# Early release of the first w_in columns, a split q normalisation and a later eighth block in a fused attention and feed-forward kernel

## The chip, the cores and the metric

The kernel runs on one core of one Trainium2 chip. Times are microseconds of the device (us); a lower time is better. The engines are named as in the profile: PE is TensorE, PEld its weight loads, DVE is VectorE, ACT is ScalarE, POOL is GpSimd, SP is SyncE, which here issues transfers only.

## What is computed

The reference is a linear attention followed by a feed-forward layer. q, k and v are (8 batches, 8 heads, 576 positions, 64) in f32; the result is (4608, 512) in f32.

```python
q_s = softmax(q, axis=-1)          # over the 64 of a head
k_s = softmax(k, axis=2)           # over the 576 positions
kv  = einsum('bhsd,bhse->bhde', k_s, v)
x   = einsum('bhsd,bhde->bhse', q_s, kv)   # then (4608, 512): positions x (heads, 64)
h   = x @ w_in                     # (4608, 2048)
g   = h + sin(alpha * h)**2 / (alpha + 1e-9)
out = g @ w_out                    # (4608, 512)
```

## The kernel before

**Tiles.** The 4608 rows are cut into nine tiles of 512 (index t), so a batch of 576 rows is one tile and an eighth; a batch is held as nine blocks j of 64 rows. The 2048 columns of w_in are 16 blocks ni of 128; the contraction over 512 has four steps ki. xT holds the attention's result transposed (four chunks c of 128 partitions), win and wout the weights in bf16.

**Attention of a batch.** `exp_q` and `exp_k` take the exponentials on ACT in two halves ii (line 117, 128 x 1152 each). `norm_q` sums q's exponentials (144), takes reciprocals (145) and multiplies (146); its list of engines says who multiplies which half, and sums and reciprocals are always DVE's. The normalised q is transposed: in batch 0 by PE through an identity matrix (186), with ACT copying the result to qT (325, 334, 335). `kv_mm` multiplies k's exponentials with v and a column of ones (157), `kv_norm` divides on DVE into kbd (167, 170), and `attn_chunk` (214) multiplies kbd with qT into xT, which ACT and DVE copy in turn (342).

**Feed-forward of a tile.** `h_slot` runs four matmuls for a block ni (234), the sine on ACT (240), the square on ACT (242), POOL (244) or DVE (246) by a string of letters, and the combination on DVE (250). Then `o_quad` (tile 0) or `o_stream` multiplies with wout (254) and copies out (260). Tile 0 starts with ki 0 and 1 of blocks 0 and 1, then goes on block by block. Its sixteen blocks take PSUM banks from two pools: four in ps_h, two lent by ps_e for blocks 2, 3, 8, 9, 14 and 15. o_quad's four accumulators take the four banks of ps_h, which the last ps_h blocks, 10 to 13, free; a ps_e tile asked for afterwards waits for block 14.

**What sets the order.** Each engine works through its own list in the order in which the code issues it, and waits for the others by semaphores; nothing is rescheduled. A transfer is started by the engine on which it is issued: SP for q, k, v, the results and (before) the first 256 columns of w_in, which come as f32 into a staging tile wf (280) and are cast by POOL (320). The other columns and w_out are issued by POOL, which casts in the transfer (107, 110). Staging tiles come from a pool of five.

**The head (before the first feed-forward matmul).** SP issues q, k, v of batch 0 and then wf's two halves, one behind the other (94, 275, 280). POOL waits for k's first half with a one-element copy called held (317), then issues six requests for w_in columns 256 to 1536, casts wf in one piece, and issues the rest. PE fills its waits with matmuls whose result is not used, `warm_up` (306): seven before batch 0's first transposes, six between the two groups of transposes. v is cast in four pieces by ACT and DVE (310). At the end of the head ACT loads the table for the sine (343).

**Around the end of tile 0.** o_quad's matmuls are drawn by `take(os, n)`. After ten of them PE computes block j 8 of batch 0 (`attn_chunk` into xp), ACT copies it (396), 36 more matmuls follow, and ACT's list goes on with batch 1's exponentials (the table for these is loaded first), then batch 1's norm_q with POOL and DVE, the k exponentials, the v casts (131) and so on.

Of the kernel before, what the change touches and what calls it, by code (L numbers as in the profile page):

```python
# [15 lines left out]
F32 = mybir.dt.float32  # L16
BF16 = mybir.dt.bfloat16
# [6 lines left out]
def kernel(  # L24
# [14 lines left out]
    nc = tc.nc  # L39
    ctx.enter_context(nc.allow_non_contiguous_dma(reason="layout"))  # L40
    B, H, S, D = q.shape
# [3 lines left out]
    J = 9  # L45
    P = S // J
# [7 lines left out]
    singles = ctx.enter_context(tc.tile_pool(name="singles", bufs=1))  # L54
    stage = ctx.enter_context(tc.tile_pool(name="stage", bufs=5))
    att1 = ctx.enter_context(tc.tile_pool(name="att1", bufs=1))
    att2 = ctx.enter_context(tc.tile_pool(name="att2", bufs=2))
# [9 lines left out]
    xT = singles.tile([128, 4, NT], BF16, name="xT")  # L67
    win = singles.tile([128, 4, d_ff], BF16, name="win")
# [7 lines left out]
    def src_view(t, b):  # L76
        return t[b].rearrange("(i e) (p j) d -> (e p) i (j d)", e=2, j=J)

    win_v = moe_w_in.rearrange("(x c d) n -> x d c n", x=2, c=4)
# [3 lines left out]
    staged = {}  # L83

    def load(name, t, b, halves=False, eng=nc.sync, gate=None):

        st = stage.tile([128, 4, J, D], F32, name=f"st_{name}", tag="st")
        for ii in range(2) if gate else ():
            gate(st[:, ii, 0, 0:1], zero)
        view = src_view(t, b)  # L90
        flat = st.rearrange("p i j d -> p i (j d)")
        if halves:
            for ii in range(2):
                eng.dma_start(out=flat[:, ii::2], in_=view[:, ii::2])  # L94
        else:
            eng.dma_start(out=flat, in_=view)
        staged[name, b] = st
# [6 lines left out]
    def load_win(c0, c1):  # L104
        n = slice(c0, c1)
        for x in range(2):
            nc.gpsimd.dma_start(out=win[64 * x:64 * x + 64, :, n], in_=win_v[x][:, :, n])

    def load_wout(c):
        nc.gpsimd.dma_start(out=wout[:, 4 * c:4 * c + 4, :], in_=wout_v[:, 4 * c:4 * c + 4, :])  # L110


    A = {}

    def exp_to(dst, src):
        for ii in range(2):
            nc.scalar.activation(dst[:, :, ii * 128:(ii + 1) * 128].rearrange("p j (x d) -> p x j d", x=2),  # L117
                                 src[:, ii::2], AX.Exp)

    def exp_q(b):  # L120
        A["qe", b] = att2.tile([128, J, 4 * D], BF16, name="qe")
        exp_to(A["qe", b], staged["q", b])

    def exp_k(b):
        A["ke", b] = att2.tile([128, J, 4 * D], BF16, name="ke")
        exp_to(A["ke", b], staged["k", b])

    def cast_v(b, engs):
        vv = vb[b % 2].rearrange("p j (i c) -> p i j c", i=4)
# [3 lines left out]
    def norm_q(b, engs):  # L133

        qe = A["qe", b].rearrange("p j (ii x d) -> p ii j x d", ii=2, x=2)
        A["qn", b] = qn = att1.tile([128, 2, J, 2 * D], BF16, name="qn")
        qs = small.tile([128, J, 4], F32, name="qs")
        if len(engs) == 1:
            nc.vector.tensor_reduce(qs, A["qe", b].rearrange("p j (i d) -> p j i d", i=4), axis=AXL.X, op=ALU.add)  # L139
            nc.vector.reciprocal(qs, qs)  # L140
        for ii in range(2):
            part = qs[:, :, 2 * ii:2 * ii + 2]
            if len(engs) == 2:
                nc.vector.tensor_reduce(part, qe[:, ii], axis=AXL.X, op=ALU.add)  # L144
                nc.vector.reciprocal(part, part)
            engs[ii % len(engs)].tensor_tensor(qn[:, ii].rearrange("p j (x d) -> p j x d", x=2), qe[:, ii],  # L146
                                               part.unsqueeze(3).to_broadcast([128, J, 2, D]), op=ALU.mult)
# [25 lines left out]
    def q_tile(b):  # L173
        if ("qT", b) not in A:
            A["qT", b] = att2.tile([128, 2, J, 128], BF16, name="qT")
        return A["qT", b]
# [6 lines left out]
    def q_transpose_ii(b, ii, j0, j1, tp):  # L183

        for j in range(j0, j1):
            nc.tensor.transpose(tp[:, j - j0], A["qn", b][:, ii, j], identb)
# [80 lines left out]
    ACT_CP, DVE_CP, GP_CP = nc.scalar.copy, nc.vector.tensor_copy, nc.gpsimd.tensor_copy  # L267
    V, GP = nc.vector, nc.gpsimd
# [5 lines left out]
    for ii, j0, j1 in VJ:  # L274
        nc.sync.dma_start(out=st[:, ii::2, j0:j1].rearrange("p i j d -> p i (j d)"),
                          in_=src_view(v, 0)[:, ii::2, j0 * D:j1 * D])

    wf = stage.tile([128, 4, J, D], F32, name="st_w", tag="st")[:, :, 0:4].rearrange("p c a b -> p c (a b)")
    for x in range(2):
        nc.sync.dma_start(out=wf[64 * x:64 * x + 64], in_=win_v[x][:, :, 0:256])  # L280
    make_identity(nc, ident)
    DVE_CP(identb, ident)
    zero = singles.tile([128, 1], F32, name="zero")
# [14 lines left out]
    nc.vector.reciprocal(inva_sb, alpha_sb)  # L298

    exp_q(0)  # L300
    exp_k(0)

    def warm_up(n):

        for _ in range(n):
            nc.tensor.matmul(warm, identb, A["qe", 0][:, 0:4, 0:128], start=True, stop=True)

    def cast_v0(ii, j0, j1, eng):
        vv = vb[0].rearrange("p j (i c) -> p i j c", i=4)
        eng(vv[:, 2 * ii:2 * ii + 2, j0:j1, 0:D], staged["v", 0][:, ii::2, j0:j1])  # L310


    warm_up(7)
    norm_q(0, [V, V])
    q_tile(0)

    GP_CP(singles.tile([128, 1], F32, name="held"), staged["k", 0][:, 0, 0, 0:1])
    for c0, c1 in ((256, 512), (512, 1024), (1024, 1536)):
        load_win(c0, c1)
    GP_CP(win[:, :, 0:256], wf)  # L320
    load_win(1536, 2048)
    for c in range(2):
        load_wout(c)
# [1 line left out]
    ACT_CP(A["qT", 0][:, 0, 0:8], tps[0])  # L325
    cast_v0(0, 0, 5, ACT_CP)
    cast_v0(0, 5, 9, DVE_CP)
    warm_up(6)
    q_transpose_ii(0, 1, 0, 8, tps[1])
    for ii in range(2):  # L330
        q_transpose_ii(0, ii, 8, 9, tps[2][:, ii:ii + 1])
# [7 lines left out]
    for c in range(4):  # L339
        xp = ps_h.tile([128, MF], F32, name="hp", tag="h")  # L340
# [4 lines left out]
    def h_slot(t, ni, sq, lag, wide=None):  # L345
        hp = mm_h(t, ni, wide, 2 if t < 2 and ni < 2 else 0)
        lag.append((t, ni, hp, sine(t, ni, hp, sq)))

    def flush(lag, keep):
        while len(lag) > keep:  # L350
            combine(*lag.pop(0))
# [14 lines left out]
    def take(it, n=1000):  # L366
        for _ in range(n):
            if next(it, 0) == 0:
                return
# [4 lines left out]
    with ES:  # L374
        def lent():
            return ps_e.tile([128, 2, MF], F32, name="hh", tag="a")[:, 0]

        late = {6: lambda: load("q", q, 1, halves=True, gate=DVE_CP), 8: lambda: load_wout(2),
                10: lambda: load_wout(3), 13: lambda: load("k", k, 1, halves=True, gate=DVE_CP)}
        for ki in range(2):  # L380
            for ni in range(2):
                mm_h(0, ni, lent, ki, ki + 1)
        for ni in range(nN):
            h_slot(0, ni, "DPAPPAPPAPPAPPAP"[ni], lag, lent)
            flush(lag, 1)
            if ni in late:
                late[ni]()
        flush(lag, 0)

        accs = [ps_h.tile([128, dm], F32, name="hp", tag="h") for _ in range(4)]  # L390
        os = o_quad(0, accs, [DVE_CP, ACT_CP, DVE_CP, ACT_CP])
        take(os, 10)
        xp = ps_e.tile([128, 4, P], F32, name="xp", tag="a")
        for c in range(4):
            attn_chunk(0, c, 8, 9, xp[:, c])
        ACT_CP(xT[:, :, 8 * P:9 * P], xp)
        take(os, 36)
        exp_q(1)
        load("v", v, 1, halves=True)
        load_batch(2)  # L400
        norm_q(1, [GP, V])
        exp_k(1)
        for ii in range(2):
            q_transpose(1, ii, ps_e, DVE_CP)
        cast_v(1, [ACT_CP, DVE_CP])
        nc.scalar.activation(zero, zero, AX.Sin)
        take(os, 8)
        kv_mm(1, 0, ps_e, split=True)
        kv_norm(1, 0, 1)
        take(os, 2)  # L410
        kv_mm(1, 1, ps_e, split=True)
        kv_norm(1, 1, 2)
        take(os, 1)

        c0 = J * P
        for ii in range(2):
            xp = ps_e.tile([128, 2, 512], F32, name="xp", tag="a")[:, :, 0:7 * P]
            for e in range(2):
                attn_chunk(1, 2 * ii + e, 0, 7, xp[:, e])
            (ACT_CP, DVE_CP)[ii](xT[:, 2 * ii:2 * ii + 2, c0:c0 + 7 * P], xp)  # L420
            take(os, 2)
        take(os)
        load("q", q, 3)
        load("k", k, 3)

        for ki in range(2):
            for ni in range(2):
                mm_h(1, ni, lent, ki, ki + 1)
        for ni in range(nN):
            h_slot(1, ni, SQ[ni], lag, lent)  # L430
            flush(lag, 1)
        cast_v(2, [GP_CP, GP_CP])
        flush(lag, 0)
# [17 lines left out]
    os = o_stream(1)  # L451
    take(os, 8)
    xp = ps_a.tile([128, 4, 2 * P], F32, name="xp", tag="a")
# [19 lines left out]
    for c in range(4):  # L473
        xp = ps_h.tile([128, MF], F32, name="hp", tag="h")[:, 0:6 * P]
# [3 lines left out]
    xp = ps_a.tile([128, 2, 512], F32, name="xp", tag="a")[:, :, 0:6 * P]  # L478
# [27 lines left out]
    for t in range(3, nT):  # L506
        b = t + 1 if t + 1 < B else None
        os = o_stream(t - 1)
# [59 lines left out]
```

The softmax here doesn't subtract the row's maximum and nothing guards it: scores larger than these inputs give would overflow.

## Time and profile before

| | us |
|---|---|
| median of five runs | 290.25 |
| the five runs | 289.45, 289.58, 290.25, 290.43, 290.51 |
| the profiled execution, its own time | 289.19 |
| its span (first to last instruction) | 287.4 |
| PE busy | 275.0 (96%) |
| ACT busy | 227.3 (79%) |
| DVE busy | 188.5 (66%) |
| POOL busy | 80.2 (28%) |
| line 234, 520 matmuls | 129.7 |
| line 254, 496 matmuls | 124.2 |

Times of single instructions come from the one profiled execution. A matmul's end is modelled, and matmuls overlap, so the distance between the starts of neighbours says more than the length of one. In a timeline line the columns are the start, the length, the engine, the line of the code, the operation, what it writes from what, and how many were merged; in brackets is the idle time before it and what ended it. In a line of waits they are the total, the number and the longest.

### The profile page before, as it was taken

The numbers are of one execution on the slowest core, as the hardware profiler recorded it, in microseconds if no ns is written. First come the engines' busy times: TensorE is split into PE (matmuls) and PEld (weight loads), VectorE is DVE, ScalarE is ACT, GpSimd is POOL, SyncE is SP. The second block draws the span as 40 slices with busy tenths as digits, with TensorE's granted clock in tenths as the row PEclk, the third lists the DMA queues.
The fourth block names the chain that finished last, engine by engine and source line by source line (L and its number), as shares of the span: only waits on it lengthen the run. The fifth ranks groups of instructions, "written<-read, shape, count | busy, mean of one in ns | idle before, by whom it ended". The sixth has DMA issues, their size and how long they took to land.

```text
span 287.4 us, 4262 instructions
## 1 busy us (share of the span) xinstructions
PE 275.0 (96%) x1570; PEld 130.4 (45%) x1570; DVE 188.5 (66%) x280; ACT 227.3 (79%) x321; POOL 80.2 (28%) x73
## 2 busy tenths in 40 slices
PE   1899999999999999999999999999999999999994
PEld 0434454445454445444544454445444444444443
DVE  3967596889958667856776677757674555555412
ACT  4799765999479999899889998999877777777500
POOL 0779420675775571005300440032000000000000
PEclk9999999999999999999999999999999999999998
DMA  7999999855899956129911990116011111111142
GB/s 253 339 203 237 271 392 407 284 197 168 189 181 410 364 185 125 38 44 366 277 34 23 329 334 6 38 39 138 17 39 37 37 37 39 37 38 37 46 104 73
DMA packets 37893, 46.03 MB, mean 160 GB/s; under 512 B 15968, under 2 KB 21360, under 8 KB 37872
## 3 DMA queue, kind: packets, MB, share of 16 engines
q1 hardware_dynamic: 33392, 41.69, 47.4%
q0 software_dynamic: 4288, 3.93, 8.4%
q8 instruction: 12, 0.20, 0.3%
q10 hardware_dynamic: 192, 0.14, 0.2%
q14 instruction: 9, 0.07, 0.1%
HBM read 36.71 MB, written 9.44 MB: 161 GB/s over the span
## 4 chain that ended last, share of the span: by engine, by line
PE 81%; DMA 5%; POOL 4%; DVE 3%; issue 2%; ACT 2%; SPq 2%; POOLq 0%
PE hp L234 35%; PE op L254 33%; PE hp L254 4%; POOL s L244 4%; DMA st_w<-in_moe_w_in_dram 3%; PE kvp L157 2%; ACT s L240 2%; PE xp L206 2%; PE hh L234 2%; DMA qT<-qn 1%; PE op L538 1%; PE op L234 1%; DVE g L250 1%; SPq L94 1%; DVE qs L144 1%
## 5 line engine op out<-in xcount | busy, mean ns | idle before, releaser
L250 DVE SCALAR_TENSOR_TENSOR g<-s,inva_sb,hp 128x512 bf16<-128x512 f32 x130 | 96.2, 745 | 64.2 <-ACT s L242 54.2
L234 PE MATMUL hp<-xT,win 128*128 128x512 bf16 x520 | 129.7, 379 | 0.3 <-POOL win L320 0.3
L254 PE MATMUL op<-wout,g 128*128 128x512 bf16 x496 | 124.2, 379 | 0.0
L240 ACT ACTIVATE s<-hp,alpha_sb 128x512 f32<-128x512 f32 x130 | 87.7, 683 | 25.4 <-PE hp L234 25.1
L234 PEld LDWEIGHTS <-win 128*128 128x128 bf16 x576 | 56.1, 98 | 68.0 <-POOL win L320 0.8
L254 PEld LDWEIGHTS <-g 128*128 128x128 bf16 x560 | 54.1, 98 | 61.4 <-issue 0.6
L242 ACT ACTIVATE s<-s 128x512 f32<-128x512 f32 x112 | 70.5, 630 | 3.6
L146 POOL TENSOR_TENSOR qn<-qe,qs 128x1152 bf16<-128x1152 bf16 x12 | 25.3, 2129 | 73.9 <-DVE qs L140 62.5
L244 POOL TENSOR_TENSOR s<-s 128x512 f32<-128x512 f32 x29 | 30.5, 1063 | 21.9 <-ACT s L240 21.4
L260 DVE COPY o<-op 128x512 f32<-128x512 f32 (+2 forms) x33 | 22.1, 669 | 9.5 <-PE op L254 7.1
L117 ACT ACTIVATE ke<-st_k 128x1152 bf16<-128x1152 f32 x16 | 17.9, 1151 | 3.0 <-DMA st_k<-in_k_dram 3.0
L117 ACT ACTIVATE qe<-st_q 128x1152 bf16<-128x1152 f32 x16 | 17.8, 1155 | 2.8 <-DMA st_q<-in_q_dram 2.8
L139 DVE TENSOR_REDUCE qs<-qe 128x36 f32<-128x2304 bf16 x5 | 12.8, 2553 | 8.7 <-ACT qe L117 8.6
L131 POOL CAST vb<-st_v 128x1152 bf16<-128x1152 f32 x12 | 13.6, 1163 | 10.4 <-DMA st_v<-in_v_dram 10.4
L254 PE MATMUL hp<-wout,g 128*128 128x512 bf16 x64 | 15.1, 379 | 0.0
L209 DVE CAST xT<-xp 128x512 bf16<-128x512 f32 (+1 forms) x18 | 13.4, 742 | 0.0
L144 DVE TENSOR_REDUCE qs<-qe 128x18 f32<-128x1152 bf16 x6 | 8.0, 1331 | 4.9 <-ACT qe L117 4.9
L117 ACT ACT_TABLE_LOAD x7 | 9.0, 1283 | 1.3 <-PEq L552 1.2
L157 PEld LDWEIGHTS <-ke 64*128 64x128 bf16 x288 | 8.2, 93 | 3.5 <-ACT s L242 1.3
L157 PE MATMUL kvp<-vb,ke 64*128 64x130 bf16 x288 | 9.7, 216 | 0.0
L234 PE MATMUL hh<-xT,win 128*128 128x512 bf16 x40 | 9.4, 379 | 0.0
L206 PE MATMUL xp<-qT,kbd 128*128 128x256 bf16 (+1 forms) x40 | 8.2, 286 | 0.4 <-DVE xT L209 0.3
(68 smaller groups left out, 116.9 us busy)
## 6 DMA issues: line engine op xcount, KB each, us to landing
out_dram<-o SPq DMA_DIRECT2D x70, 128.0 KB, 2.3
st_q<-in_q_dram SPq DMA_DIRECT2D x6, 1152.0 KB, 6.2
st_k<-in_k_dram SPq DMA_DIRECT2D x6, 1152.0 KB, 8.4
st_v<-in_v_dram SPq DMA_DIRECT2D x6, 1152.0 KB, 10.3
st_q<-in_q_dram SPq DMA_DIRECT2D x4, 576.0 KB, 5.6
st_k<-in_k_dram SPq DMA_DIRECT2D x4, 576.0 KB, 6.8
wout<-in_moe_w_out_dram POOLq DMA_DIRECT2D x4, 512.0 KB, 10.2
st_v<-in_v_dram SPq DMA_DIRECT2D x3, 576.0 KB, 9.5
```

What stands on the lines that cost most here:

```text
L117: nc.scalar.activation(dst[:, :, ii * 128:(ii + 1) * 128].rearrange("p j (x d) -> p x j d", x=2), src[:, ii::2], AX.Exp)
L131: engs[ii](vv[:, 2 * ii:2 * ii + 2, :, 0:D], staged["v", b][:, ii::2])
L146: engs[ii % len(engs)].tensor_tensor(qn[:, ii].rearrange("p j (x d) -> p j x d", x=2), qe[:, ii], part.unsqueeze(3).to_broadcast([128, J, ...
L157: nc.tensor.matmul(kvp[:, e, ii * 130:(ii + 1) * 130], ke[r, j, ii * 128:(ii + 1) * 128], vt[r, j, ii * 130:(ii + 1) * 130], start=(j == 0 ...
L206: nc.tensor.matmul(xp[:, e, 0:n], kt[:, e, ii], qT[:, ii, j0:j1, e * 64:(e + 1) * 64], start=True, stop=True)
L234: nc.tensor.matmul(hp, win[:, ki, ni * 128:(ni + 1) * 128], xT[:, ki, t * MF:(t + 1) * MF], start=(ki == 0), stop=(ki == 3))
L240: nc.scalar.activation(s, hp, AX.Sin, scale=alpha_sb[:, ni:ni + 1])
L242: nc.scalar.activation(s, s, AX.Square)
L244: nc.gpsimd.tensor_tensor(s, s, s, op=ALU.mult)
L250: nc.vector.scalar_tensor_tensor(G[t][:, ni], in0=s, scalar=inva_sb[:, ni:ni + 1], in1=hp, op0=ALU.mult, op1=ALU.add)
L254: nc.tensor.matmul(acc, G[t][:, ni, j * 128:(j + 1) * 128], wout[:, ni, :], start=(ni == 0), stop=(ni == nN - 1))
L260: eng(o[:, cols], acc)
```

## The change

Four edits in the head and one after tile 0:

- the two transfers of wf are no longer issued behind v: ACT writes one element of wf between the two halves of k's exponentials, and SP's transfers, which overwrite wf, wait for that. The copy held is gone, and POOL's requests for the other columns stand behind its share of norm_q;
- norm_q of batch 0 multiplies its first half on POOL and its second on DVE, instead of both on DVE;
- POOL casts wf in two pieces of 128 columns each;
- the warm-up matmuls are nine and one instead of seven and six;
- block j 8 of batch 0 comes after twenty matmuls of o_quad instead of ten, and DVE copies it instead of ACT; 26 follow instead of 36.

```diff
@@ -112,8 +112,8 @@
 
     A = {}
 
-    def exp_to(dst, src):
-        for ii in range(2):
+    def exp_to(dst, src, iis=(0, 1)):
+        for ii in iis:
             nc.scalar.activation(dst[:, :, ii * 128:(ii + 1) * 128].rearrange("p j (x d) -> p x j d", x=2),
                                  src[:, ii::2], AX.Exp)
 
@@ -121,9 +121,10 @@
         A["qe", b] = att2.tile([128, J, 4 * D], BF16, name="qe")
         exp_to(A["qe", b], staged["q", b])
 
-    def exp_k(b):
-        A["ke", b] = att2.tile([128, J, 4 * D], BF16, name="ke")
-        exp_to(A["ke", b], staged["k", b])
+    def exp_k(b, iis=(0, 1)):
+        if 0 in iis:
+            A["ke", b] = att2.tile([128, J, 4 * D], BF16, name="ke")
+        exp_to(A["ke", b], staged["k", b], iis)
 
     def cast_v(b, engs):
         vv = vb[b % 2].rearrange("p j (i c) -> p i j c", i=4)
@@ -276,8 +277,6 @@
                           in_=src_view(v, 0)[:, ii::2, j0 * D:j1 * D])
 
     wf = stage.tile([128, 4, J, D], F32, name="st_w", tag="st")[:, :, 0:4].rearrange("p c a b -> p c (a b)")
-    for x in range(2):
-        nc.sync.dma_start(out=wf[64 * x:64 * x + 64], in_=win_v[x][:, :, 0:256])
     make_identity(nc, ident)
     DVE_CP(identb, ident)
     zero = singles.tile([128, 1], F32, name="zero")
@@ -298,7 +297,12 @@
     nc.vector.reciprocal(inva_sb, alpha_sb)
 
     exp_q(0)
-    exp_k(0)
+    exp_k(0, (0,))
+
+    nc.scalar.copy(wf[:, 0, 0:1], zero)
+    exp_k(0, (1,))
+    for x in range(2):
+        nc.sync.dma_start(out=wf[64 * x:64 * x + 64], in_=win_v[x][:, :, 0:256])
 
     def warm_up(n):
 
@@ -310,14 +314,13 @@
         eng(vv[:, 2 * ii:2 * ii + 2, j0:j1, 0:D], staged["v", 0][:, ii::2, j0:j1])
 
 
-    warm_up(7)
-    norm_q(0, [V, V])
+    warm_up(9)
+    norm_q(0, [GP, V])
     q_tile(0)
-
-    GP_CP(singles.tile([128, 1], F32, name="held"), staged["k", 0][:, 0, 0, 0:1])
     for c0, c1 in ((256, 512), (512, 1024), (1024, 1536)):
         load_win(c0, c1)
-    GP_CP(win[:, :, 0:256], wf)
+    for n in range(2):
+        GP_CP(win[:, :, n * 128:n * 128 + 128], wf[:, :, n * 128:n * 128 + 128])
     load_win(1536, 2048)
     for c in range(2):
         load_wout(c)
@@ -325,7 +328,7 @@
     ACT_CP(A["qT", 0][:, 0, 0:8], tps[0])
     cast_v0(0, 0, 5, ACT_CP)
     cast_v0(0, 5, 9, DVE_CP)
-    warm_up(6)
+    warm_up(1)
     q_transpose_ii(0, 1, 0, 8, tps[1])
     for ii in range(2):
         q_transpose_ii(0, ii, 8, 9, tps[2][:, ii:ii + 1])
@@ -389,12 +392,12 @@
 
         accs = [ps_h.tile([128, dm], F32, name="hp", tag="h") for _ in range(4)]
         os = o_quad(0, accs, [DVE_CP, ACT_CP, DVE_CP, ACT_CP])
-        take(os, 10)
+        take(os, 20)
         xp = ps_e.tile([128, 4, P], F32, name="xp", tag="a")
         for c in range(4):
             attn_chunk(0, c, 8, 9, xp[:, c])
-        ACT_CP(xT[:, :, 8 * P:9 * P], xp)
-        take(os, 36)
+        DVE_CP(xT[:, :, 8 * P:9 * P], xp)
+        take(os, 26)
         exp_q(1)
         load("v", v, 1, halves=True)
         load_batch(2)
```

## The prediction

> **What bounds the kernel now.** I read the page first: PE is busy 96% of the span, so only what keeps PE waiting, and what PE does before its stream begins, can move the time. Then the list of PE's waits over the whole span (us in total, times, longest), without its first two lines, 3.1 and 2.8 for the first transfers:
>
> ```profile
> ...
> PE tp L186 <- DVE qn L146: 1.0, 1, 1.0
> PE hp L214 <- DVE kbd L170: 0.6, 2, 0.4
> PE hp L234 <- POOL win L320: 0.3, 1, 0.3
> PE xp L206 <- DVE xT L209: 0.3, 1, 0.3
> PE xp L214 <- DVE g L250: 0.3, 1, 0.3
> ```
>
> All but the last two lie in the head, before the first feed-forward matmul. The chain that ended last shows what starts that stream:
>
> ```profile
> 5.82 9.17 DMA st_w<-in_moe_w_in_dram
> ...
> 15.12 1.05 POOL win L320
> ...
> 16.22 1.90 PE hp L234 x8
> ```
>
> The first w_in columns land at 14.99, GpSimd casts them for 1.05, and PE starts at 16.22. From there it runs at one 512-column matmul per 0.216 us ((1.90 - 0.38) / 7), and the only waits left are 0.3 and 0.3. But the timeline shows a second chain just behind it:
>
> ```profile
> 14.88 0.59 ACT L342 CAST xT<-hp 128x512 bf16<-128x512 f32 x1 [0.15 <-PE hp L214]
> 15.27 1.36 DVE L342 CAST xT<-hp 128x512 bf16<-128x512 f32 x2
> ...
> 15.72 0.59 ACT L342 CAST xT<-hp 128x512 bf16<-128x512 f32 x1 [0.25 <-PE hp L214]
> ...
> 16.32 1.28 ACT L343 ACT_TABLE_LOAD   x1
> ```
>
> xT's four chunks are done at 15.47, 15.95, 16.31 and 16.63, so the columns are ahead of need by only half a microsecond. And ACT goes from its last copy straight into the sine table, then sines (the first at 17.73). The table of busy time by stretch (PE, PEld, DVE, ACT, POOL after the length) says that ACT is full in this stage:
>
> ```profile
> 25.00:30.00 5.00, 5.00 (x25) 2.25 (x23) 4.00 (x6) 4.80 (x8) 4.97 (x6) 1.00 1.15 294
> ```
>
> So the first tile has two limits: PE from 16.22, and ACT from 16.32, which nowhere in it waits for PE. They meet here:
>
> ```profile
> 30.05 2.42 PE L254 MATMUL hp<-wout,g 128*128 128x512 bf16 x10
> ...
> 32.75 0.28 PE L214 MATMUL xp<-qT,kbd 128*128 128x64 bf16 x4 [0.28 <-DVE g L250]
> ```
>
> Ten matmuls from 30.05 would be through the issue at 30.05 + 10 x 0.216 = 32.21; xp starts at 32.75. That is 0.54 lost: about 0.1 inside the ten (2.42 against 9 x 0.216 + 0.38 = 2.32: the fourth accumulator's bank, freed by the sine of column block 13), 0.44 for xp, whose buffer the combine of block 14 frees.
>
> **What the Trainium skill says.** GPSIMD Engine Reference, section 4.1: a two-input elementwise operation takes GpSimd about twice VectorE's time. Here the same multiplication takes 2.13 on POOL and 1.36 on DVE, a ratio of 1.6. Its section 1 says that GpSimd shares SBUF interfaces with VectorE, contended when DVE has two SBUF inputs. The trace agrees; line 146 on DVE alone, and beside POOL in batch 1:
>
> ```profile
> 7.83 1.36 DVE L146 TENSOR_TENSOR qn<-qe,qs 128x1152 bf16<-128x1152 bf16 x1
> ...
> 37.77 2.13 POOL L146 TENSOR_TENSOR qn<-qe,qs 128x1152 bf16<-128x1152 bf16 x1 [5.34 <-DVE qs L145]
> ...
> 39.14 1.97 DVE L146 TENSOR_TENSOR qn<-qe,qs 128x1152 bf16<-128x1152 bf16 x1
> ```
>
> DMA: Bandwidth & Descriptors, section "Queues, rings and completion order": descriptors start in order on a ring, and an engine takes turns between rings by packets. The trace agrees: w_in lands after v on SP's queue, and from 13.0 to 13.5 the two queues share:
>
> ```profile
> q1 hardware_dynamic: 87, 0.08, 74.5%
> q0 software_dynamic: 59, 0.03, 44.1%
> ```
>
> TensorE: Matmul & The Clock Gate, Part 1: PE starts at half clock and gets the full one after a busy window of about 3.4 us. Here the seven warm-ups run 0.43 apart (3.14 - 0.63 over 6 gaps) and six later ones 0.216 apart ((1.46 - 0.38) / 5).
>
> **The change, part by part.**
> *Release of the first columns.* The one-element ACT copy costs 0.20 (nearest row: the L343 activation, 0.20). It lies between the first k exponential (ends 9.28) and the second, which waited 0.27 for its DMA until 9.55, so it costs nothing; without that cover 0.2 on ACT. SP's two requests move from 5.01 to about 9.55 and end near 11.0 (1.46 for both); the next request on SP is at 24.6, so nothing queues behind them. On the ring they still follow v, whose last piece lands at 12.9, so the late request isn't felt if bytes flow about a microsecond after it (the first q request, at 0.74, had bytes moving by 2.0). "held" (1.09 on POOL) goes. GpSimd's requests start when its multiplication ends, near 10.1 instead of 9.17; its first bytes, at 12.8 before, come near 13.7. So the columns travel almost alone. Bounds: landing at 13.9 (v's end plus 1 us) to 14.99 (nothing gained); I take 14.4. POOL's six requests (4.07) end at 14.2, just in time. The cast in two: by the rows of 1152 and 1024 elements (1.16, 1.04) 512 cost 0.56, so blocks 0 and 1 are ready at 15.0 and 15.6.
> *q's first half on GpSimd.* As in batch 1, relative to the first reciprocal (7.80 here, 37.60 there): POOL 7.97 to 10.10; DVE's second half no longer stands behind the first, so reduce 7.7 to 9.0, reciprocal to 9.3, product 9.3 to 11.3 (1.97, beside POOL) instead of to 12.14. First transposes 10.15 instead of 9.24; ACT's qT copy 10.85 instead of 10.62, its v cast ends 12.5 instead of 12.25. Second transposes end at 12.0. The first kv matmul is then held by that v cast: 12.55 instead of 12.86, a gain of 0.3. kbd's first half: 14.1 instead of 14.4. The second kv half stays at the end of v (12.9, cast to 13.55, 14.07), but DVE is then free, so its reciprocal is at 14.1 instead of 14.43. All xT copies, the table load and ACT's whole stage move by 0.3. If POOL's product is seen 0.3 later, this gain is 0; it can't exceed 0.37 (14.43 - 14.06).
> *Warm-ups.* Nine and one instead of seven and six; they fill waits. PE's stream starts at about 15.35 (xT chunk 0 at 15.25): 0.85 earlier.
> *Block j 8 later, on DVE.* xp after 20 matmuls is about 2 us past its buffer's release: the 0.44 goes. DVE's copy costs about 0.4 (ACT's row: 0.37) ahead of batch 1's reduce, which still starts earlier, because ACT's exponentials start at 32.3 to 33.7 instead of 34.75.
> *Where the stalls go.* In tile 0 PE's 0.85 isn't kept: accumulator 4 depends on ACT, which gives 0.3. Then 0.44, so PE is 0.74 ahead at about 34. Next late is batch 1's v:
>
> ```profile
> 41.66 1.17 ACT L131 CAST vb<-st_v 128x1152 bf16<-128x1152 f32 x1 [0.21 <-DMA st_v<-in_v_dram]
> ...
> 43.50 0.68 PE L157 MATMUL kvp<-vb,ke 64*128 64x130 bf16 x18
> ```
>
> The cast ends at 42.83 and follows a DMA; PE, 0.74 earlier, would be there at 42.76. With queues busy as before and GpSimd's later start passed on by 0.1 to 0.2, PE waits about 0.24. After that PE has no waits of size but its own. Sum: 0.30 + 0.44 - 0.24 = 0.50. The profiled execution took 289.19 (span 287.4, 1.8 around it), which goes to 288.7. The median shown is 290.25, 1.06 above the profiled one; I take the difference off it: 289.75.
>
> **Rivals.** *ACT isn't a limit* (for: PE shows no wait from 16.2 to 30; against: ACT 4.8 of 5): PE keeps 0.85 + 0.54 - 0.24 = 1.15, to 289.1. *The gain is lost*: the columns land no earlier, POOL's product costs the 0.3, or batch 1's v comes later by all of 0.4: 290.2. *Slower, by the clock*: three warm-ups fewer, and short transposes where six stood; if the clock isn't granted by the end of the nine (6.16 + 9 x 0.43 = 10.0; before it came by 9.24), PE enters the stream at half rate. Half a window of 3.4 us is 1.7, plus 0.4 for the kv and xT matmuls, less 0.5: 291.85. For: between 10.0 and 15.35 PE has only some 3 us of work. Against: it was granted 3.1 us after the first warm-up. *The edits don't do what they say*: the instruction order shows that they do.
>
> **How the numbers follow.** Likeliest 0.47 (289.4 to 290.1), PE keeps the head 0.19, gain lost 0.20, clock 0.14. A measurement of this kernel can tell 0.3%, 0.87 us. Faster by that: most of the second case and a tail of the first, 0.25; slower: the clock and a little of the lost case, 0.16; within: 0.59. The range leaves out the clock's case and the far end of the second: 288.6 to 291.0.
>
> **What would show it.** Right: the first win cast before 15.2, L234's start near 15.4, ACT's table load at 16.0, no xp wait, DVE's L146 at about 1.97, a new small wait at batch 1's kv. Wrong: columns landing at 15, ACT waiting for PE in tile 0, L234 0.43 apart.

## The result and the profile after

The changed kernel takes 292.11 us (median of 23 executions, 289.87 and up) against 289.88 for the kernel before on the same chip (42 executions): a ratio of 1.0081, 95% interval 1.0066 to 1.0096. On a second chip it was 291.74 against 289.75, 1.0055 (1.0029 to 1.0081). One execution of 593 us, far from all the others, is no part of the ratio. The forecast was 289.75; the kernel became slower by 2.2 us where 0.5 was to be gained.

The profiled execution took 293.85 (span 292.0). PE's waits after the change (us in total, times, longest), without the two for the first transfers:

```profile
PE kvp L158 <- ACT vb L314: 2.2, 2, 1.6
PE hp L235 <- POOL win L323: 0.9, 1, 0.9
...
```

The wait of xp for the combine (0.3 in this list before) is gone. In its place stand 2.2 us for v's casts at the first kv matmuls, and 0.9 instead of 0.3 for the first columns. The chain that ended last shows these columns (start, length, what):

```profile
9.53 0.09 ACT st_w L302
...
9.64 0.76 SPq L305
...
10.44 6.77 DMA st_w<-in_moe_w_in_dram
...
17.36 0.62 POOL win L323
18.03 2.02 PE hp L235 x4
```

The columns land at 10.44 + 6.77 = 17.21 (14.99 before; 14.4 was forecast), and PE's stream starts at 18.03 (16.22 before). The chain now begins at the new release, and no longer at a request of 5 us. The timeline of the same execution shows what happened on PE (start, length, engine and line, count, idle time ahead of it and releaser):

```profile
12.61 1.03 PE L158 MATMUL kvp<-vb,ke 64*128 64x130 bf16 x28 [0.63 <-ACT vb L314]
15.24 0.40 PE L158 MATMUL kvp<-vb,ke 64*128 64x130 bf16 x8 [1.61 <-ACT vb L314]
...
16.55 0.60 PE L215 MATMUL hp<-qT,kbd 128*128 128x512 bf16 x2 [0.37 <-DVE kbd L171]
18.03 0.61 PE L235 MATMUL hp<-xT,win 128*128 128x512 bf16 x1 [0.87 <-POOL win L323]
```

Between 13.64 and 18.03 PE has some 1.5 us of work. What that leads to is in the table of busy time by stretch, cut here every 3.41 us (length, then PE, PEld, DVE, ACT and POOL, then PE's granted clock, DMA share, GB/s):

```profile
10.25:13.66 3.41, 2.47 (x47) 1.89 (x46) 2.16 (x5) 2.31 (x3) 3.41 (x6) 1.00 1.15 264
13.66:17.08 3.42, 1.47 (x12) 0.45 (x11) 1.79 (x6) 2.39 (x5) 0.21 (x1) 1.00 1.20 192
17.08:20.49 3.41, 2.54 (x7) 0.84 (x7) 0.81 (x2) 1.97 (x3) 3.13 (x6) 0.50 1.24 205
20.49:23.91 3.42, 3.42 (x9) 1.21 (x8) 1.72 (x3) 1.79 (x3) 1.74 (x2) 0.50 1.18 166
23.91:27.30 3.39, 3.39 (x17) 1.52 (x16) 1.95 (x3) 3.06 (x6) 1.80 (x2) 1.00 1.16 173
```

After the stretch in which PE worked for 1.47 of 3.42 us, the clock is halved for exactly two more: nine matmuls in 3.42 us at 20.49, seventeen at 23.91. The sum: PE starts 1.81 later; from 18.03 to 23.91 it runs at half rate, which loses (23.91 - 18.03) / 2 = 2.94; xp's wait gives 0.44 back. That is 4.3 of the 4.6 us between the spans (292.0 and 287.4).

Not every execution loses the clock. On the second chip 8 of 18 executions had a mean granted clock under 0.997 (median 293.59); the ten at full clock had 290.67, still 1.02 above the full-clock median of before (289.65). So there are two things to explain: about a microsecond that is always lost, and three that are lost when the clock goes. (Full clock means here a mean granted clock of 0.997 or more. This mean counts from the first grant on: a grant that comes late in the head doesn't show in it.)

### The profile page after: what moved, and what is told of

Read it like the earlier page. It is cut to its first block, busy times and chain, and to the rows that moved or that the text cites. A ratio compares the mean times of both kernels' runs of the same rounds, so it can differ in the third digit from the quotient of the medians.

```text
span 292.0 us, 4259 instructions
## 1 busy us (share of the span) xinstructions
PE 277.9 (95%) x1567; PEld 131.3 (45%) x1567; DVE 188.1 (64%) x280; ACT 227.1 (78%) x321; POOL 81.2 (28%) x74
## 4 chain that ended last, share of the span: by engine, by line
PE 87%; DMA 6%; DVE 2%; issue 1%; ACT 1%; SPq 1%; POOL 1%; POOLq 0%
PE hp L235 38%; PE op L255 34%; PE hp L255 5%; PE hh L235 3%; PE kvp L158 2%; DMA st_w<-in_moe_w_in_dram 2%; DMA st_k<-in_k_dram 2%; PE xp L207 2%; DMA qT<-qn 1%; PE op L541 1%; PE op L235 1%; DVE qs L145 1%; DVE o L261 0%; PE xp L215 0%; ACT s L241 0%
## 5 line engine op out<-in xcount | busy, mean ns | idle before, releaser
L235 PE MATMUL hp<-xT,win 128*128 128x512 bf16 x520 | 131.5, 383 | 0.9 <-POOL win L323 0.9
L235 PEld LDWEIGHTS <-win 128*128 128x128 bf16 x576 | 56.9, 99 | 70.7 <-issue 3.7
L147 POOL TENSOR_TENSOR qn<-qe,qs 128x1152 bf16<-128x1152 bf16 x13 | 27.4, 2127 | 78.9 <-DVE qs L141 62.3
L210 DVE CAST xT<-xp 128x512 bf16<-128x512 f32 (+1 forms) x18 | 13.4, 742 | 0.0
L235 PE MATMUL hh<-xT,win 128*128 128x512 bf16 x40 | 10.6, 414 | 0.0
```

Source lines behind the costliest of these rows:

```text
L235: nc.tensor.matmul(hp, win[:, ki, ni * 128:(ni + 1) * 128], xT[:, ki, t * MF:(t + 1) * MF], start=(ki == 0), stop=(ki == 3))
```

## The experiments

The first theory after the result was that the late request of the columns is the whole cost. Its rivals: GpSimd's product costs, or PE loses its clock for want of warm-ups. Runs under one heading shared a chip and the runs of before; between headings only the ratios to before are compared, and shares of lowered clocks with caution.

### The parts, first series (before: 290.52, median of 47; 13 of them with a lowered clock)

**e1: the change without the late release.**

```
+    for x in range(2):
+        nc.sync.dma_start(out=wf[64 * x:64 * x + 64], in_=win_v[x][:, :, 0:256])   # behind v, as before
...
-    exp_k(0, (0,))
-    nc.scalar.copy(wf[:, 0, 0:1], zero)
-    exp_k(0, (1,))
-    (the two requests)
+    exp_k(0)
```

> The changed kernel with one edit taken back: the first w_in columns are again requested on SP straight behind v, at about 5 us, with no element of wf written by ACT; all else stays changed. Theory 'late release' (the requests made at 9.6 put the columns, and v's last piece with them, among GpSimd's bytes, and the wait that follows drops PE's clock): v's last piece lands at 12.9 again, the columns by 15, PE's line 235 starts near 15.5 and stays at 0.216 us a matmul; 289.2 to 289.7, slightly faster than before. Rival 'warm-ups' (three fewer drop the clock): still 2 us slower than before, with matmuls 0.43 apart after the start. Rival 'GpSimd's product' (the normalisation holds v's cast and GpSimd's requests): still over 291.

Measured: 291.24 against 290.52, 1.002 (0.9991 to 1.0048). A smaller ratio than the whole change's (1.0055 and 1.0081), but not the gain that the theory promised (289.2 to 289.7). Whether something else costs, this run leaves open, since its interval holds 1; f1 and g1 decide it.

**e2: the late release alone, in the kernel before.**

> The kernel before with the release alone: ACT writes one element of wf between k's two exponentials and SP requests the first w_in columns after that; GpSimd's copy named held, both products on VectorE, warm-ups 7 and 6, one cast, block j 8 as before. 'Late release': v's last piece lands past 13.5, the columns past 16, the line 234 stream starts past 17; 291.5 to 293. 'Warm-ups': 290.0, as before, for the thirteen warm-ups are there. 'GpSimd's product': 290.0.

Measured: 295.71, 1.016 (1.0112 to 1.0207), worse than the whole change. Here GpSimd's first request (9.46) stands ahead of SP's (9.87), and its bytes move from 11.44: the second half of the columns lands at 18.83. PE's list of waits:

```profile
PE hp L235 <- POOL win L323: 3.9, 1, 3.9
```

All six executions had the clock lowered, in the profiled one from 18.94 to 25.77. This is the largest loss of any run here. In g3 below, where SP's requests stand at 7.31 and so ahead of GpSimd's (8.83), the kernel before with block j 8 moved loses nothing: request time and order changed together, so the two runs don't tell which of them counts.

**e3: the change with the old warm-ups, 7 and 6.**

> The changed kernel with the warm-up matmuls of before, seven and six. 'Late release': no help, since they are over by 11.5 and the clock falls in the wait after 13: 292, and some executions with the clock halved for 3.4 us or twice that. 'Warm-ups': 289.5, no halved clock after 13. 'GpSimd's product': 292.

Measured: 291.88, 1.0054 (1.0027 to 1.008). The clock was lowered in 6 of 18 executions, in the first runs of the changed kernel in 18 of 22 (f0 below: 8 of 18); at full clock the median is 291.41, where the kernel before has 290.11 in this series. So the six warm-ups may keep the clock more often (the chips differ), and don't mend the loss. In the profiled execution the clock was granted only at 14.36 (9.18 before), and the six took 2.77 us instead of 1.46.

**e4: j 8 alone (taken after 20, copied by VectorE).**

```
-        take(os, 10)
+        take(os, 20)
...
-        ACT_CP(xT[:, :, 8 * P:9 * P], xp)
-        take(os, 36)
+        DVE_CP(xT[:, :, 8 * P:9 * P], xp)
+        take(os, 26)
```

> The kernel before with block j 8 of batch 0 alone moved: after twenty matmuls of the quad instead of ten, copied by VectorE. All theories: the 0.44 us wait before xp goes, and up to half of it comes back at batch 1's first kv; 0.2 to 0.45 us faster than before. If PE's gain there is all taken by a later wait, 0.

Measured: 290.27, 0.9968 (0.9943 to 0.9994): a gain, but one that the ratio makes out of the lowered clocks (3 of 22 executions, 13 of 47 of before); at full clock the medians are 290.06 and 290.11. In its timeline xp follows the twentieth matmul with no wait, and the wait that the prediction had announced appears at batch 1's v, longer than said, and longer than what xp had waited:

```profile
30.73 4.58 PE L254 MATMUL hp<-wout,g 128*128 128x512 bf16 x20
35.15 0.28 PE L214 MATMUL xp<-qT,kbd 128*128 128x64 bf16 x4
...
44.71 0.69 PE L157 MATMUL kvp<-vb,ke 64*128 64x130 bf16 x18 [0.94 <-ACT vb L131]
```

### The release and the queues, second series (before: 289.75)

**f0: the changed kernel again.**

> The changed kernel itself, beside its variants on the same chip: 0.6 to 1.0% slower than before, most executions with a halved clock somewhere after 13 us (a mean clock of 0.994 or less).

Measured: 291.74, 1.0055 (1.0029 to 1.0081). Its profiled execution kept the clock, and so shows the always lost microsecond by itself (PE's timeline):

```profile
14.01 0.40 PE L158 MATMUL kvp<-vb,ke 64*128 64x130 bf16 x8 [0.65 <-ACT vb L314]
...
17.16 0.39 PE L235 MATMUL hp<-xT,win 128*128 128x512 bf16 x1 [1.25 <-POOL win L323]
17.72 1.69 PE L235 MATMUL hp<-xT,win 128*128 128x512 bf16 x7 [0.17 <-POOL win L323]
```

The columns' second half landed at 16.34, three microseconds after v's last piece (13.31). PE starts 0.94 later than before and loses 0.34 at the second matmul (0.56 apart instead of 0.22); less 0.44 for xp that is 0.84 of the 1.2 us between the spans. And why this one kept its clock (columns as above):

```profile
8.76:12.17 3.41, 2.28 (x23) 1.25 (x21) 2.90 (x5) 3.14 (x5) 3.41 (x5) 1.00 1.08 367
12.17:15.59 3.42, 2.19 (x40) 1.28 (x39) 2.19 (x8) 2.42 (x5) 1.73 (x3) 1.00 1.29 199
15.59:19.00 3.41, 2.00 (x9) 0.70 (x8) 1.06 (x2) 2.10 (x4) 2.50 (x5) 1.00 1.22 201
```

Its clock was granted at 8.76 instead of 10.25, so stretches of 3.41 us cut PE's gap elsewhere, and none has less than 2.00 of work.

**f1: early request and old warm-ups, so the change without two of its five parts.**

> The changed kernel with two edits taken back: the first columns requested behind v at 5 us, and the warm-ups seven and six. 'Late release' with 'warm-ups' as its second part (release makes the head 1.3 us longer at full clock; nine and one warm-ups let more executions fall to half clock): 290.0, at or below before, and no more executions with a lowered clock than before. If GpSimd's product costs by itself, 290.8 with the clock full.

Measured: 290.64, 1.0025 (1.0008 to 1.0042). It stays slower than before, which leaves GpSimd's product as a cost (the half casts are a term of 0.1, and block j 8 is no loss in e4): the theory that only the release costs has fallen.

**f3: the change, with GpSimd's requests held until v's last piece is there.**

```
+    GP_CP(singles.tile([128, 1], F32, name="held"), staged["v", 0][:, 1, 8, 0:1])
     for c0, c1 in ((256, 512), (512, 1024), (1024, 1536)):
         load_win(c0, c1)
```

> The changed kernel with one wait more: GpSimd copies an element of v's last piece before it requests the other columns, so its requests come after v, near 13.5 to 14.5. Theory 'sharing' (the late request lets GpSimd's bytes go between v's last piece and the first columns): v's last piece and the second half of the first columns land earlier than in the changed kernel, at about 13 and 14.5, with a rate of over 300 GB/s from 12 to 13; but the other columns come too late and PE waits at block 2, so the time is about as bad. Rival 'lateness' (a request at 9.6 is itself slow, whoever else is there): the second half lands past 16 as in the changed kernel.

Measured: 294.04, 1.0149 (1.0125 to 1.0173), all four executions with the clock lowered. GpSimd's timeline says why:

```profile
13.77 0.19 POOL L320 COPY held<-st_v 128x1 f32<-128x1 f32 x1 [4.04 <-DMA st_v<-in_v_dram]
13.90 3.88 POOL L107 DMA_DIRECT2D win<-in_moe_w_in_dram  x6
17.73 1.22 POOL L324 CAST win<-st_w 128x512 bf16<-128x512 f32 x2
```

The columns landed at 14.99, but their cast stands behind six requests until 17.73. As a repair it fails; as a measurement it shows, in one execution, that neither the late request nor GpSimd's product (7.61 to 9.74 here) is a harm as such: with GpSimd's queue silent the columns come 1.27 after v's last piece, in the changed kernel 2.67 (17.21 less 14.54). The DMA queues of the changed kernel from 12 to 14 (packets, MB, share of the engines):

```profile
q1 hardware_dynamic: 232, 0.22, 67.5%
q0 software_dynamic: 238, 0.11, 52.8%
```

The same two microseconds in f3:

```profile
q1 hardware_dynamic: 375, 0.35, 81.2%
```

In the changed kernel GpSimd's queue (q0) has as many packets as SP's (q1), and SP's moves 0.22 MB instead of 0.35.

**f4: the change, with the release ahead of both k exponentials, so that SP's requests stand at 7.4 and 8.2.**

```
-    exp_k(0, (0,))
-
     nc.scalar.copy(wf[:, 0, 0:1], zero)
-    exp_k(0, (1,))
+    exp_k(0)
```

> The changed kernel with ACT's write ahead of both of k's exponentials, so that SP requests the first columns near 7.7 and 8.4, still behind v on the ring but 2 us ahead of GpSimd. 'Sharing': the columns stand in the ring before GpSimd's bytes, v's last piece and the columns land as when requested at 5; about 1 us faster than the changed kernel. 'Lateness' by itself: between the two. If only the wait itself counts, no difference from the changed kernel.

Measured: 290.12, 1.0015 (0.9997 to 1.0033), 1.6 us under the changed kernel of the same series, and 5 of 22 executions with a lowered clock (8 of 18). At full clock it gains 0.7 (289.96 against 290.67). Two microseconds of request time, with all else the same, are most of what the change loses. Through what, the profile does not show. From 12 to 14 GpSimd's queue is indeed kept off, with 38 packets (238 in the changed kernel's profile, 261 in f0's). But v's last piece lands at 14.16 (13.31 in f0) and the columns at 16.18, hardly before f0's 16.34: a packet of SP's queue takes 0.097 us here, 0.088 in f0 and 0.062 in the kernel before. And with the columns requested at about 5 they land at 16.31 in e1 and 16.24 in f1. So where GpSimd has the product, the late request explains only what lies past 16.3; the section on the prediction returns to this.

### The other parts alone, third series (before: 289.90)

**g1: GpSimd's product alone** (early request, warm-ups 7 and 6, ACT's j 8 as before).

```
-    norm_q(0, [V, V])
+    norm_q(0, [GP, V])
     q_tile(0)
-    GP_CP(singles.tile([128, 1], F32, name="held"), staged["k", 0][:, 0, 0, 0:1])
```

> The kernel before with GpSimd's product alone: the first half of batch 0's q normalised on GpSimd, whose requests for the other columns then stand behind it, so the copy held is left out. First columns requested at 5, warm-ups 7 and 6, one cast, block j 8 as before. If this edit costs by itself (the two variants with an early request were 0.25 and 0.2% slower than before): 290.4 against 289.75, at full clock. If its cost is the warm-ups' and the two casts': within 0.1% of before.

Measured: 290.77, 1.0038 (1.0021 to 1.0055). The product was to gain 0.3 us and costs 1.1 (0.38%). POOL in its profiled execution:

```profile
7.89 2.13 POOL L146 TENSOR_TENSOR qn<-qe,qs 128x1152 bf16<-128x1152 bf16 x1 [6.59 <-DVE qs L145]
9.96 3.90 POOL L107 DMA_DIRECT2D win<-in_moe_w_in_dram  x6
16.48 1.04 POOL L319 CAST win<-st_w 128x1024 bf16<-128x1024 f32 x1 [2.62 <-DMA st_w<-in_moe_w_in_dram]
```

POOL is free for the cast at 13.9 and waits 2.62 for columns that SP asked for at 4.65; they land at 16.35 (14.99 before). But PE shows no wait for them in this execution, for its own chain is as late:

```profile
10.90 2.77 PE L306 MATMUL warm<-qe,identb 128*128 128x512 bf16 x6
13.46 1.27 PE L186 MATMUL tp<-identb,qn 128*128 128x128 bf16 x10
14.66 1.34 PE L157 MATMUL kvp<-vb,ke 64*128 64x130 bf16 x36
```

PE had waited 0.83 for the product before the first transposes, the clock was granted only at 15.02, and until then the six warm-ups and the transposes behind them ran at half rate: kv starts at 14.66 instead of 12.86. So g1 prices the product, and leaves open whether it costs through the columns or through a late grant; h3 takes the six warm-ups away.

**g2: warm-ups 9 and 1 alone.**

> The kernel before with the warm-up matmuls nine and one instead of seven and six, nothing else. 'Warm-ups drop the clock': the share of executions with a mean clock under 0.997 goes from about one in ten to a third or more, and the median up by 0.3 to 0.8 us. If the clock falls only through the long wait for the columns: no difference from before.

Measured: 289.57, 0.9999 (0.998 to 1.0017). No effect within 0.2%.

**g3: j 8 as in e4, with the early release of f4, in the kernel before.**

> The kernel before with two edits: block j 8 later and on VectorE (alone 0.3% faster), and the first columns released by an ACT write ahead of k's exponentials, at about 7.5, two microseconds ahead of GpSimd. Late release costs only when GpSimd's bytes get ahead of the columns, so: as with block j 8 alone, 0.2 to 0.4% faster than before. If any delay of the request costs: no faster than before.

Measured: 289.32, 0.9981 (0.9968 to 0.9994), no execution of 22 with a lowered clock. It beats both kernels, and at full clock too (289.31 against 289.79). Next to f4 it also prices the product, the half casts and 9/1 together once more: 1.0015 less 0.9981 is 0.34%.

**g4: the change, with six warm-ups between the halves of the kv loop.**

> The changed kernel with six more warm-up matmuls (1.3 us) between the two halves of batch 0's kv, where PE waits for v's last piece. If the clock falls because PE has too little work from about 13.5 to 17: hardly any execution with a lowered clock, and the median falls from 291.7 to the full-clock value of the changed kernel, 290.7. If the clock is lost otherwise: the same share of lowered clocks as the changed kernel, eight in eighteen, and 291.7 or above.

Measured: 291.31, 1.0046 (1.0026 to 1.0066). Half a hit: the clock was lowered in 3 of 22 executions, with 3.03 us of PE work from 13.4 to 16.8; but the full-clock median is 291.24, not the 290.7 expected. What filler saves in clock does not become time here.

### Why GpSimd's product costs, fourth series (before: 289.70)

Without the one-element copy, GpSimd does 2.1 us of work at 7.8 and its requests come at 9.9. Either could delay the transfers.

**h1: the kernel before, its one-element copy reading k's second half** (requests at 9.59, GpSimd idle).

> The kernel before, with the copy held reading k's second half instead of its first, so that GpSimd's requests start about 1.5 us later, near 10.7. If later requests cost (the other columns come late, or meet v): 0.3% slower or more. If the cost of GpSimd's product is its work beside v's transfers or PE's chain: within 0.15% of before.

Measured: 290.01, 1.0011 (0.9997 to 1.0024); columns at 15.02.

**h2: the kernel before, two copies of half of q's exponentials to a tile that nothing reads, in place of the one-element copy.**

> The kernel before, with two GpSimd copies of q's exponentials (128 x 1152 each, 1.2 us) into a spare tile in place of the copy held; nothing reads the spare tile. GpSimd is busy from about 7.6 to 9.9 and its requests follow, as with the product; both products stay on VectorE. If GpSimd's activity beside v's transfers costs: 0.3% slower, with v's last piece at 14. If PE's chain is what costs: within 0.15% of before.

Measured: 290.78, 1.0026 (1.0011 to 1.0041); columns at 16.14. Its requests stood at 10.77, VectorE's first product took 2.17 instead of 1.36, and the clock was granted only at 13.89, so three more things had changed than I wanted.

**h3: g1 with warm-ups 9 and 1.**

> The kernel with GpSimd's product alone (g1) and the warm-ups nine and one. If the product's cost is the hole in PE's warm-ups and the six that stand ahead of the second transposes: most of the 0.38% goes, 290.0 against 289.9. If it is v's arrival: it stays, 290.6.

Measured: 290.92, 1.0041 (1.0026 to 1.0056), so the cost stays. In the profiled execution the clock was granted at 9.32, the columns landed at 16.10 and PE waited 0.5 for them: here it is the transfers that are late, v's last piece (14.19) with them. 8 of 22 executions had a lowered clock, against 1 of 14 for g1 on another chip; the warm-ups, harmless alone, may be missed once the gap behind them has grown.

### Requests or work, fifth series (before: 289.94)

**i1: requests later, GpSimd idle; i2: one spare copy, requests as early as before; i3: the one-element copy reading k's second exponential.**

```
-    GP_CP(singles.tile([128, 1], F32, name="held"), staged["k", 0][:, 0, 0, 0:1])
i1 +    GP_CP(held[0], staged["k", 0][:, 1, 0, 0:1])
i1 +    GP_CP(held[1], held[0])
i1 +    GP_CP(held[2], held[1])
i2 +    GP_CP(singles.tile([128, 9, 128], BF16, name="spare"), A["qe", 0][:, :, 128:256])
i3 +    GP_CP(singles.tile([128, 1], BF16, name="held"), A["ke", 0][:, 0, 128:129])
```

> The kernel before, with GpSimd's six requests at about 9.9 instead of 9.2: its one-element copy reads k's second half and is followed by two more one-element copies, each of the one ahead, so that the engine is otherwise idle. 9.9 is where the requests stand in the changed kernel and in the run with the product alone. If the moment of the requests decides (later than about 9.7 is too late), the first columns land at 16.1 or later, SP's packets take 83 ns or more between 12 and 14, and the ratio is about 1.003. If GpSimd's work decides, they land by 15.7 with packets of 60 to 70 ns, ratio 1.000 to 1.001.

Measured: 291.17, 1.003 (1.001 to 1.005). The requests came at 11.97 and not at 9.9: the third copy, of one element a partition, took 1.36. The columns landed at 16.28.

> The kernel before, with one copy of half of q's exponentials to a spare tile, read by nothing, in the place of the one-element copy: GpSimd is busy from about 7.5 to 9.1, and its requests stand at 9.1 as before. If GpSimd's work beside the transfers decides, the columns land at 16.1 or later and the ratio is about 1.0025, as with two copies. If the moment of the requests decides, they land by 15.7 and the ratio is 1.000.

Measured: 290.95, 1.0035 (1.0019 to 1.005). Requests at 8.74, columns at 16.19.

> The kernel before, with the one-element copy reading the second half of k's exponentials: GpSimd is idle until about 10.8, and its requests stand where they stood with two spare copies (10.8). If the moment of the requests decides, this run is as that one: columns at 16.1, ratio about 1.0025. If GpSimd's work decides: columns by 15.7 and a ratio near 1.000, unless requests at 10.8 cost something of their own later in w_in's stream.

Measured: 292.04, 1.0078 (1.0047 to 1.0108). Requests at 11.84, but the columns were there before the cast could start: it stands behind the requests until 15.77.

i2 speaks against the requests' moment as the only cause of late columns, and so does i3 against i1: requests within 0.15 us of each other, columns at 15.02 in one and at 16.28 in the other. Each is one execution, and the same kernel's columns landed 0.87 apart (17.21, and 16.34 in f0). GpSimd's work goes with late columns in every profile that has it at 7.5 to 10 and an early or middling request of SP's (e1, f1, f4, g1, h2, h3, i2: 16.1 to 16.4, against 14.8 to 15.7 in before, e4, g2, g3, h1, i3), but i1 is late without it, and f3, with the product and no requests of GpSimd's until 13.90, has them at 14.99. Work without requests is thus not enough. And in i2 and h2 VectorE's stretched product moves all of q's path by 0.8, which costs something of its own. That the product costs 0.4% is shown twice (g1, h3); that it does so through late transfers is supported by h3, with a late grant of the clock beside it in g1; by what mechanism the transfers are late is open.

## Why the prediction was wrong, step by step

**"The late request isn't felt … the columns travel almost alone": this step failed.** It had GpSimd's first bytes at 13.7, worked out as if they would keep their place behind the columns, and the columns at 14.4. But SP's second request was not through until 11.07 (9.64 + 1.43), and GpSimd's began at 9.92. GpSimd's bytes started at 12.39, before v's last piece was there (14.54), and the two queues shared the engines until the columns landed at 17.21. Where the columns are requested earlier and the product is the same, 13.7 is about right: GpSimd's first bytes came at 13.4 to 13.9, and its queue moved 9 to 80 packets from 12 to 14 (e1, f1, f4, g1, h3). Where they are requested late (the changed kernel, f0, e3, g4), it was 12.3 to 12.6, and 153 to 261 packets. The section of the Trainium skill that I cited, DMA: Bandwidth & Descriptors, "Queues, rings and completion order", says just this (an engine takes turns between rings), and the DMA table of before showed the sharing from 13.0; I used the number and not the rule. What showed it: f3 (queue silent, columns at 14.99), e2 (GpSimd's requests first, 18.83), and in time, though not in the landing of its one profile, f4 (two microseconds earlier, 1.6 us of the median). The columns' delay has a second part, which comes with the product and is there at an early request too (16.1 to 16.4). My own bound, 14.99, was too narrow: it took "nothing gained" for the worst case.

**v's last piece at 12.9: failed, as a reading of one execution.** It landed between 12.13 and 14.54 in the profiles here, at 14.16 in e4, which changes nothing ahead of it, and at 13.31 (f0) and 14.54 in the changed kernel itself. The second kv half was put at 13.55 and came at 15.24. Executions differ by more than the whole margin that I argued over.

**The product on GpSimd, a gain of 0.3: failed.** Its local terms were right (POOL 2.13 from 7.85 to 9.98, VectorE's half 1.95 from 9.25, first kv at 12.61 against 12.55), and the whole costs 0.38% (g1), 0.41% (h3). The terms were all of engines; that the transfers under way would come later was not in the sum, and neither was the clock's grant, which came at 15.02 in g1 after PE's wait of 0.83 for the product (at 8.79 in f1, with the same head on PE: not in every execution).

**The warm-ups "fill waits": right alone (g2), wrong in company.** The rival had the loss of clock right and its place wrong: the clock was granted at 10.25, when the nine had ended, and lost at 17.08, with little work of PE's ahead of it (1.47 us of 3.42). It was priced at one window of 3.4 us at half rate, a loss of 1.7, and took two windows, a loss of 2.94.

**ACT as the second limit: reached only at full clock, and later than said.** In the changed kernel's profiled execution, with the clock halved, ACT waits for PE in tile 0 (its list of waits):

```profile
ACT s L241 <- PE hp L235: 2.2, 3, 1.9
ACT s L241 <- PE hh L235: 1.0, 1, 1.0
```

This was named ahead as a sign of a wrong prediction, and so was L235 at 0.43 apart. The table load came at 17.58 and not at 16.0. In f0, at full clock, ACT waits for PE once, 1.2 before its first sine (at 19.01; 17.73 before), and not again in the tile: there the limit holds, but PE's late start decides when it sets in.

**j 8: right in its mechanism, unsure in its size.** xp no longer waits, in e4 and in the changed kernel. Of the 0.44 little is kept in e4: the new wait at batch 1's kv is there as forecast, with 0.94 instead of 0.24. The ratio of e4 (0.06 to 0.57% gained) and its full-clock medians (0.05 us) differ; with the early release beside it (g3) 0.5 us are gained by either. In the changed kernel that wait does not appear; PE comes there at 47.77 instead of 43.50.

**The two half casts:** 0.61 each in place of 0.56, a pair of 1.17 where the whole took 1.05. A term of 0.1.

The parts add up as far as they can: product +0.38%, warm-ups 0, j 8 between 0 and -0.32%, and two microseconds of the late release +0.40% (f0 less f4), together 0.46 to 0.78%, where 0.55 and 0.81% were measured. It is a rough sum: each part comes with an interval of about 0.2 to 0.3 to either side, and product and release act on the same transfers.

**A reading that was the wrong way round.** The columns were not "ahead of need by only half a microsecond". Their cast ended at 16.17, and xT's first two chunks, all that the first four matmuls take, were there at 15.95: PE waited for the columns, as its 0.3 in the list says. They were ahead of xT's last chunk only (16.63).

## What to carry to other kernels

When a request is moved later "behind work that hides it", ask which other queue's requests it now falls behind or beside: in the kernel here the early place was what kept the other queue off, and it was lost with the delay. Take no landing time from one profile for a margin of a microsecond: here the same kernel's columns differed by 0.87 between two executions, and v's last piece by 1.23. And where a step leaves PE idle ahead of its stream, count PE's work in stretches of a clock window: waits of two microseconds in one such stretch cost three more here. The moment of the grant differs from execution to execution (9.18 and 11.84 with the same head in the kernel before and in e4), so the same gap may cost nothing in one and three microseconds in the next.

## What the runs showed that I had not expected

**The clock goes by work in a window, not by idleness alone.** In every profile of a loss in the head or in tile 0, the 3.41 us that ended with it held at most 1.87 us of PE work (1.47 in the changed kernel, 1.87 in e1, 1.70 in f1, 1.61 in f4 and i3, 1.37 in f3, 0.60 in e2), and PE never stood idle for a whole one. Every window with 2.00 or more (f0) kept the clock. Between the two there is no clean line: g2 kept it with 1.66, h3 with 1.73, f3 once with 1.81, i2 with 1.92, and busy times rest on modelled ends. The way back is sharper: half-rate windows with 2.26 (e2), 2.54 (the changed kernel), 2.58 (g1), 2.59 (e3) and 2.66 (h2) did not bring the full clock, those with 2.71 (f0), 2.81 (f1), 2.97 (f3) and more did. The ones of g1, e3, h2, f0 and f1 lie in the head: PE's wait before the first transposes (0.83 in g1) took the windows of g1, e3 and h2 under that line (2.58 + 0.83 = 3.41), and PE stayed at half rate for one window more. The Trainium skill, TensorE: Matmul & The Clock Gate, Part 1, has a free-running window of about 3.4 us and a fall after an idle one; the length agrees (10.25 to 17.08 and on to 23.91 are two each), and "idle" is here a window in which PE was busy for up to 1.87 us.

**A one-element copy on GpSimd can take as long as VectorE's product beside it.** The timeline of POOL in i1:

```profile
10.43 0.19 POOL L319 COPY held<-held 128x1 f32<-128x1 f32 x1
10.67 1.36 POOL L320 COPY held<-held 128x1 f32<-128x1 f32 x1
```

The timeline of DVE in the same execution:

```profile
10.63 1.36 DVE L146 TENSOR_TENSOR qn<-qe,qs 128x1152 bf16<-128x1152 bf16 x1
```

The same copy takes 0.19 ahead of the product and 1.36 under it, until it ends; the copy of 1.09 in the kernel before had run under one too. The other way round, a spare copy that had started first stretched the product from 1.36 to 2.18 (i2). The Trainium skill, GPSIMD Engine Reference, section 1, says that the two share SBUF interfaces and contend when VectorE has two SBUF inputs; in these runs the one that started second took longer by nearly what was left of the other.

**SP's packets take longer in the late executions.** From 12 to 14 a packet of SP's queue took 0.062 us in the kernel before (79.6% of 16 x 2 us, 409 packets) and 0.094 in g1, whose DMA queues in that stretch are:

```profile
q1 hardware_dynamic: 389, 0.37, 114.1%
q0 software_dynamic: 9, 0.00, 1.7%
```

Ahead of 12 us there is no such difference, and GpSimd's queue moves next to nothing here. In f3, with the product but no requests of GpSimd's yet, a packet took 0.069 (81.2%, 375 packets). Why is open.
